# Fused attention, Fourier mixing and feed-forward on one core: the planned cost of the late weight loads, the order of the last chunk, and the planner's constants

## The chip, the cores and the metric

The kernel runs on one core of a Trainium2 chip. The metric is the device time of one execution in microseconds (us). The profile names the engines of the core PE (TensorE, matrix products), PEld (its weight loads, beside PE), DVE (VectorE), ACT (ScalarE), POOL (GpSimd) and SP (SyncE, which here only issues DMAs; SPq is its queue).

## What is computed

Windowed attention over 8 batches, 8 heads, 576 positions and 64 columns a head (half of the heads see the last 32 positions, half every fourth of the last 128), then a two-dimensional Fourier transform whose real part is added, a normalisation over the 512 columns, and a feed-forward block 512 to 2048 to 512 with a residual:

```
scores = where(masks, q @ k.T / sqrt(D), -1e9);  x = softmax(scores) @ v   # heads joined: [8, 576, 512]
X = fft(fft(x, axis=1), axis=2)
u = x + real(X)
un = (u - mean(u)) / sqrt(var(u) + 1e-6)
out = u + relu(un @ w_ch1) @ w_ch2
```

The weights arrive in double precision and are taken apart on the chip. Products that need more than PE's single pass are made of a high and a low half of each operand, in three passes (`PASSES`).

## The kernel before

**An order made while the program is built.** Nothing is issued where the Python text stands. Every operation is given to `add` with its engine, a planned duration, what it reads and writes, and a priority number. At the end `Plan.run` plays the whole program through: at each moment a free engine takes, of its operations whose inputs are there in the plan, the one with the lowest number. The order so found on each engine is the program; on the chip each engine follows it strictly and waits on semaphores. For a DMA the planner counts the issuing engine's cost, a transfer of `nbytes / 2.6e5` us that follows the one before it, some 2.5 us of landing, and at most eight in flight for an engine. So a wrong planned duration does not change what is computed, but puts operations in an order that does not fit the chip. The constants `P_...` and `T_...` are offsets of these priorities (or earliest times) for each kind of work; 12 units of priority stand for one batch of attention in the first half.

**First half.** For each batch b, attention runs over four pairs of heads (`attend_pair`, three blocks each; q, k and v loaded by SP into 3 `tq`, 3 `kb` and 4 `vt` buffers). `mix` does the Fourier part and the normalisation of a batch, at priority 12(b+1) + `P_MIX` + `P_MS[b]` - 10, spread over `P_SPAN` + `P_SS[b]` - 10 units (batches 0 and 1 have their own). `prep_w` loads and takes apart the first 6 of 16 slices of the weights (`wa1`, `wa2`), at `P_W` + 9.45 f. `fill` is the feed-forward of tokens through these 6 slices in the plain way (`up` at L1026, `down` at L1042); its results go through ACT into one of two `row` buffers (`keep_part`, L1060) and by SP to memory (L1061). It is the work that can stand in wherever PE has nothing else.

**Second half.** The other 10 slices are taken two by two, in 5 pairs (`NPAIR`), with a scheme of 7 products in place of 8 for a product of 2 x 2 blocks. `blocks` prepares 14 block sums a pair. 30 of the 70 lie in `right_w` and `left_w`. The other 40 have no room as long as the first half runs: they are written to memory (L1011), and loaded late (the list `later`, L1014), 16 into `late_w` and 24 over the used `wa1` and `wa2`. The tokens come in 9 chunks of 512 (`NCH`). `load_blocks` builds the 7 combinations `xb` of a chunk. `two_tiles(p)` runs the 7 products of pair p into one PSUM bank (`product`, L1365, in the order w1; w0, w4; w5, w2; w6; w3), with a snapshot by ACT after each group (`snap`, L1373), and makes of them 7 operands for the way down (`operand`: ACT L1387, then DVE L1390 or L1394). These lie in 8 seats used in turn: 6 `h` buffers and the two `row` buffers. `down7` is one item of the way down: operand i, one half of the rows, three matmuls (L1473) into the shared sum i, one of seven, each in a PSUM bank; the sums collect over the 5 pairs. Between the groups of products `lower(n)` puts the next n items of the pair before into the program, `LOW` = (3, 3, 3, 3, 2) of its 14. Each matmul group of an item takes a turn, 0.01 of priority, and a product stands `P_UP` turns ahead of its place.

**End of a chunk.** After the last pair, `gather` (L1462) adds shared sums into u2 = s0 + s5, u3 = u2 + s6, u2 = u2 + s4. `finish` makes each of the four output tiles of 128 rows: one DVE instruction over 512 columns (L1105, from u3, or from s0's copy and u2), two over 256 (L1109, from s3 and s4, or s1 and s2), and the stores (L1122 for the last chunk, on SP and ACT). In the last chunk the items of the last pair run in the order `END` = (0, 5, 6, 4, 3, 1, 2), else `ORDER` or `FIRST`.

The planner's figures for one late load, and for SP in general:

```
P * 2048 * ROW          # 262144 bytes, ROW = 0.52
def dma(fn, r, w, prio, nbytes, cost=0.4)
```

## Time and profile before

| | us |
|---|---|
| median of 3 runs | 1077.5 (1075.42 to 1081.26) |
| the profiled execution | 1077.81 |
| its span, first to last instruction | 1076.0 |
| PE busy | 1035.3 (96%) |
| DVE busy | 893.0 (83%) |
| ACT busy | 623.9 (58%) |
| mean granted clock of PE | 0.986 |

Busy times are of the whole span; DMA moved 158 MB at a mean of 147 GB/s. A stretch in which PE is not busy, or in which its granted clock is 0.5, is time that something else than the amount of its work decides. Instruction times are from the profiler; the ends of matmuls are modelled, so that neighbouring matmul groups overlap a little in a timeline: six matmuls of 256 columns follow each other in 0.72 us and are shown with 0.87.

### The profile page before, as it was taken

What the parts mean: (1) busy time and instruction counts of PE and PEld (TensorE: products, weight loads), DVE (VectorE), ACT (ScalarE), POOL (GpSimd) and SP (SyncE); (2) the same over time, 40 slices, a digit from 0 to 9 for tenths busy, and PEclk for the clock granted to TensorE, in tenths of its full rate; (3) what the DMA queues carried; (4) which work ended last, traced back from release to release, by engine and by line L of the source; (5) the groups of instructions that cost most, each with busy time, mean ns of one, the idle gap of its engine ahead of it and who ended that gap; (6) DMA issues with size and microseconds to landing.
All of it is one profiled execution on the core that took longest, in us unless ns stands there. A gap on an engine that the chain in (4) does not pass through costs nothing.

```text
span 1076.0 us, 22711 instructions
## 1 busy us (share of the span) xinstructions
PE 1035.3 (96%) x7876; PEld 965.3 (90%) x7876; DVE 893.0 (83%) x2847; ACT 623.9 (58%) x1588; POOL 211.4 (20%) x278
## 2 busy tenths in 40 slices
PE   7999889999999899999999989999999999999996
PEld 5788679888889798999898889999999999999996
DVE  6689997887878957669988468999898999989886
ACT  5788783657845233345445356666665757565763
POOL 1034405354453445400000000000000000110010
PEclk9899999999999999999999989999999999999998
DMA  9887973675735325254778953323324242333031
GB/s 263 257 267 229 269 207 104 175 227 158 208 92 180 93 79 153 69 168 137 239 250 246 371 137 69 99 60 109 79 80 99 70 114 65 99 80 98 22 108 51
DMA packets 116451, 158.19 MB, mean 147 GB/s; under 512 B 11032, under 2 KB 64472, under 8 KB 116336
## 3 DMA queue, kind: packets, MB, share of 16 engines
q1 hardware_dynamic: 112752, 148.03, 47.8%
q0 software_dynamic: 3040, 8.09, 2.6%
q8 instruction: 62, 1.02, 0.4%
q10 hardware_dynamic: 544, 0.62, 0.2%
q14 instruction: 53, 0.43, 0.1%
HBM read 108.40 MB, written 48.29 MB: 146 GB/s over the span
## 4 chain that ended last, share of the span: by engine, by line
PE 58%; DVE 11%; DMA 5%; ACT 1%; issue 1%; SPq 0%; POOL 0%; DVEq 0%; ACTq 0%
PE ff L1365 16%; PE ff L1026 7%; PE ff L1042 7%; PE mix L1473 5%; PE sc L1473 5%; PE pt L1473 2%; PE ff L1473 2%; PE sc L1042 2%; PE av L1473 2%; PE mix L848 2%; PE av L1026 1%; PE pt L1026 1%; PE mix L802 1%; DMA late_w<-wt 1%; PE sc L586 1%
## 5 line engine op out<-in xcount | busy, mean ns | idle before, releaser
L600 ACT ACTIVATE pm<-pm,mx 96x128 f32<-96x128 f32 x384 | 129.0, 394 | 35.8 <-DVE mx L594 34.7
L1082 POOL DMA_INDIRECT ut<-us,flip_sb x20 | 27.9, 1395 | 543.2 <-ACT h L1387 181.0
L1026 PE MATMUL ff<-ut,wa 128*128 128x256 f32 x936 | 125.5, 286 | 4.3 <-DVE h L1034 4.3
L1026 PEld LDWEIGHTS ff<-ut,wa 128*128 128x128 f32 x936 | 117.5, 191 | 6.3 <-DVE h L1034 4.9
L586 PE MATMUL sc<-kb,tq 128*96 128x256 f32 x384 | 109.6, 398 | 8.1 <-DMA tq<-in_q_dram 5.7
L1042 PE MATMUL ff<-wa,h 128*128 128x512 f32 x468 | 113.0, 392 | 0.0
L594 DVE CUSTOM_DVE_ANT_0 pm<-sc,mask_sb 96x128 f32<-96x128 f32 x384 | 92.3, 280 | 24.2 <-PE sc L586 20.6
L1042 PEld LDWEIGHTS ff<-wa,h 128*128 128x128 f32 x468 | 85.7, 188 | 16.3
L620 PEld LDWEIGHTS av<-vt,ptsb 128*96 128x96 f32 x672 | 69.2, 168 | 16.4 <-issue 4.5
L1148 DVE STREAM_TRANSPOSE ut<-ut 128x512 f32<-128x512 f32 (+1 forms) x76 | 72.5, 983 | 9.9 <-DMA ut<-us 9.6
L620 PE MATMUL av<-vt,ptsb 128*96 128x65 f32 x672 | 72.5, 250 | 7.2 <-DVE xt L632 6.4
L1365 PE MATMUL ff<-xb,left_w 128*128 128x256 f32 x486 | 70.2, 286 | 8.1 <-ACT sb L1373 6.8
L1365 PE MATMUL ff<-xb,wa 128*128 128x256 f32 x540 | 75.7, 281 | 0.5 <-ACT s L1373 0.5
L586 PEld LDWEIGHTS sc<-kb,tq 128*96 128x96 f32 x384 | 55.6, 170 | 19.8 <-issue 5.8
L1365 PEld LDWEIGHTS ff<-xb,left_w 128*128 128x128 f32 x486 | 63.2, 192 | 9.4 <-ACT sb L1373 7.0
L1365 PEld LDWEIGHTS ff<-xb,wa 128*128 128x128 f32 x540 | 68.3, 188 | 0.7 <-ACT s L1373 0.7
L1365 PE MATMUL ff<-xb,late_w 128*128 128x256 f32 x486 | 68.2, 279 | 0.0
L1387 ACT ACTIVATE h<-s 128x256 fp32r<-128x256 f32 x136 | 55.4, 415 | 16.8 <-DVE s L1403 8.5
L1032 ACT ACTIVATE h<-ff 128x256 fp32r<-128x256 f32 x78 | 29.9, 383 | 55.8 <-PE ff L1026 54.5
L1365 PEld LDWEIGHTS ff<-xb,late_w 128*128 128x128 f32 x486 | 61.8, 188 | 0.1
L1060 ACT COPY row<-ff 128x512 f32<-128x512 f32 x26 | 15.2, 586 | 65.1 <-PE ff L1042 53.1
L1034 DVE SCALAR_TENSOR_TENSOR h<-ff,h 128x256 fp32r<-128x256 f32 x78 | 32.7, 419 | 23.1 <-ACT h L1032 22.7
(247 smaller groups left out, 2631.5 us busy)
## 6 DMA issues: line engine op xcount, KB each, us to landing
vt<-in_v_dram SPq DMA_DIRECT2D x32, 390.0 KB
wst<-in_w_dram SPq DMA_DIRECT2D x20, 512.0 KB
wt<-wst SPq DMA_DIRECT2D x40, 256.0 KB
us<-uc SPq DMA_DIRECT2D x36, 257.0 KB
part<-row SPq DMA_DIRECT2D x36, 256.0 KB
ut<-us SPq DMA_DIRECT2D x36, 256.0 KB
ut<-part SPq DMA_DIRECT2D x36, 256.0 KB
kb<-in_k_dram SPq DMA_DIRECT2D x62, 144.0 KB
```

The source lines that it names most:

```text
L586: nc.tensor.matmul(sc()[:QB, 256 * n:256 * n + 256], lhsT=tq()[:, cols], rhs=kb()[:, :, keys], start=True, stop=True,)
L594: nc.vector.tensor_tensor_reduce(pm()[:, i], sc()[:QB, KB * i:KB * i + KB], mask_sb()[:, masks[blocks[i // 2]]], -0.125, 3.0e38, ALU.add, ...
L600: add("ACT", 0.295, lambda i=i: nc.scalar.activation(out=pm()[:, i], in_=pm()[:, i], func=AF.Exp, bias=mx()[:, i:i + 1], scale=-1.0), ((mx ...
L620: add("PE", 0.17, lambda i=i: nc.tensor.matmul(av()[:QB, 65 * i:65 * i + 65], lhsT=pt()[:, i], rhs=vt()[:, i % 2, blocks[i // 2]], start=T ...
L1026: nc.tensor.matmul(z()[:, :n_tok], lhsT=wf()[:, a, kk], rhs=ut()[:, p, kk], start=(kk == 0 and n == 0), stop=(kk == KT - 1 and n == 2),)
L1032: add("ACT", act(n_tok) - 0.03, lambda: nc.scalar.activation(out=h()[:, 0, :n_tok], in_=z()[:, :n_tok], func=AF.Relu), (z,), ((h, 0),), prio)
L1034: add("DVE", dve(n_tok), lambda: nc.vector.scalar_tensor_tensor(h()[:, 1, :n_tok], z()[:, :n_tok], 0.0, h()[:, 0, :n_tok].bitcast(F32), op ...
L1042: nc.tensor.matmul(acc(), lhsT=h()[:, a, P * s:P * s + P], rhs=wf()[:, p], start=(first and n == 0), stop=(last and n == 2),)
L1148: nc.vector.transpose(out=o[back], in_=x[:, g])
L1365: nc.tensor.matmul(up_bank()[:, lo:lo + TOK1], lhsT=ap()[:, a, kk], rhs=xb()[:, j, p, kk], start=(start and k == 0), stop=(k == 5), skip_g ...
L1387: add("ACT", act(TOK1), lambda: nc.scalar.activation(out=ap()[:, 0], in_=src(), func=AF.Relu if relu else AF.Copy), need, (k0,), prio)
L1473: nc.tensor.matmul(acc()[:, TOK1 * half:TOK1 * half + TOK1], lhsT=ap()[:, a, P * half:P * half + P], rhs=wap()[:, q_].rearrange("p k f -> ...
```

## The change

Three things. The late loads (the list `later`) are planned with 0.66 of their bytes in place of 0.52, and with 0.65 us of SP in place of 0.4. In the last chunk the way down of the last two pairs is put together: the pair before the last lowers only its items 0, 6, 4, 5 among the last pair's products (`LOW_END`, two at a time), the last pair's items 0, 6, 5, 4 follow, and then the items 3, 2, 1 of both pairs, one sum after the other. For this the last pair's operands get seven seats of their own, over weights that are not read again. `finish` is taken apart into `end_rows`, `end_sum` and `end_store`, and each output tile gets its terms as the sums come. And some twenty constants of the planner have new values, in both halves. `T_WS` is zero everywhere and delays nothing.

```diff
-P_OP, P_GA, P_LB, P_FI = 2.43, 48.72, -40.68, 47.3
-P_PR = 128.43
-P_UP = 10.35
+P_OP, P_GA, P_LB, P_FI = -15.86, 49.21, -18.09, 56.16
+P_PR = 127.84
+P_UP = 0.2
+T_WS = [0, 0, 0, 0, 0, 0]
-P_SS = [10, 10, 10, 10, 15, 12, 10, 10]
+P_SS = [10, 10, 14, 10, 15, 12, 8, 10]
 LOW = (3, 3, 3, 3, 2)
+LOW_END = (2, 2, 2, 2, 0)
-END = (0, 5, 6, 4, 3, 1, 2)
+HEAD, HEAD_LAST, TAIL = (0, 6, 4, 5), (0, 6, 5, 4), (3, 2, 1)
 FIRST = (0, 6, 5, 3, 4, 1, 2)
...
-P_ST, P_FD, P_WD, P_ST0, P_FD0, P_SPAN0, P_SPAN1 = -4.0, -8.83, -10.91, 0.0, 0.0, 30.0, 18.9
-P_QK, P_V, P_TR, P_MIX, P_SPAN, P_W, P_WF, P_FILL, P_FILLT = -8.0, -5.24, -5.0, 4.32, 9.95, 30, 9.45, 42.52, 12.2
+P_ST, P_FD, P_WD, P_ST0, P_FD0, P_SPAN0, P_SPAN1 = -2.25, -8.83, -10.91, 0.0, 0.0, 30.0, 12.02
+P_QK, P_V, P_TR, P_MIX, P_SPAN, P_W, P_WF, P_FILL, P_FILLT = 12.68, -5.24, -5.0, -5.7, 9.95, 24.8, 9.45, 49.31, 12.2
-T_SEQ, T_CHN, T_STEP, P_SEQ, P_CHN = 10.36, 24.62, 1.0, -4.0, -2.0
+T_SEQ, T_CHN, T_STEP, P_SEQ, P_CHN = 11.54, 24.59, 1.0, -4.0, -2.0
...
-                (there, gate3) if of is late_w else (there,), ((of, ("b", x, 0)), (of, ("b", x, 1))), prio, P * 2048 * ROW))
+                (there, gate3) if of is late_w else (there,), ((of, ("b", x, 0)), (of, ("b", x, 1))), prio, P * 2048 * 0.66, 0.65))
...
+    def end_rows(idx, seat, more, half, prio):
+        t, key, at = seat
         need, get = more
 
         def rows():
+            return at()[:, 0:C].rearrange("p (n d) -> p n d", n=2)
         add("DVE", 0.66, lambda: nc.vector.scalar_tensor_tensor(
+            rows(), get(half), at()[:, C + 1:C + 2], rows(), op0=ALU.mult, op1=ALU.add), need, ((t, ("w", key)),), prio, port=True)
+
+    def end_sum(seat, n, acc, half, before, prio):
+        t, key, at = seat
+        cs = slice(256 * n, 256 * n + 256)
+        add("DVE", 0.36, lambda: nc.vector.scalar_tensor_tensor(
+            at()[:, cs], acc()[:, 256 * half:256 * half + 256], at()[:, C + 1:C + 2], at()[:, cs], op0=ALU.mult, op1=ALU.add),
+            (acc, *before), ((t, ("w", key)), (t, ("done", key, n))), prio)
+        return ((t, ("done", key, n)),)
...
+    def spare_seat(n):
+        of, i, ap = seats[n][:3]
+        return (of, ("b", i, 0)), (of, ("b", i, 1)), lambda: ap().rearrange("p a k f -> p a (k f)")
+
+    last_seats = len(hs_)
+    hs_ += [spare_seat(n) for n in range(7)]
...
+        if c == NCH - 1 and i:
+            x = 0 if i in (1, 2) else 2
+            if i == 5:
+                gather(u2, p1, s[5])
+                gather(u3, u2, s[6])
+            elif i == 4:
+                gather(u2, u2, s[4])
+            if i in (4, 2):
+                for half in range(2):
+                    end_rows(4 * c + x + half, w_of[4 * c + x + half], top_rows if i == 2 else low_rows, half, soon())
+            if i in (1, 2, 3, 4):
+                done = ()
+                for half in range(2):
+                    w = w_of[4 * c + x + half]
+                    done = end_sum(w, i % 2 == 0, s[i], half, done, soon())
+                    if i in (1, 3):
+                        end_store(4 * c + x + half, w)
+            return
...
+            def items(p, got, some, c=c):
+                return [lambda i=i, half=half: down7(c, p, i, got[i], half) for i in some for half in (1, 0)]
+            if c < NCH - 1 or p < NPAIR - 2:
+                todo += items(p, got, ORDER if p else FIRST)
+            elif not ending:
+                todo += items(p, got, HEAD)
+                kept = got
+            else:
+                todo += items(p, got, HEAD_LAST)
+                for i in TAIL:
+                    todo += items(p - 1, kept, (i,)) + items(p, got, (i,))
+        lower(len(todo) if c == NCH - 1 else 0)
```

## Rows read from the trace of the kernel before

**Rows 1.** The page, busy us of each engine, share of the span, instructions

```profile
PE 1035.3 (96%) x7876; PEld 965.3 (90%) x7876; DVE 893.0 (83%) x2847; ACT 623.9 (58%) x1588; POOL 211.4 (20%) x278
```

**Rows 2.** Windows: start:end, length, busy of each engine (instructions), clock, DMA share, GB/s

```profile
0.00:50.00 50.00, 41.73 (x264) 31.55 (x264) 32.52 (x223) 31.16 (x89) 5.75 (x14) 0.93 0.91 259
...
50.00:100.00 50.00, 48.71 (x385) 41.48 (x386) 45.15 (x267) 43.04 (x127) 14.18 (x20) 1.00 0.85 256
...
100.00:150.00 50.00, 42.46 (x312) 34.43 (x311) 48.20 (x263) 40.04 (x114) 19.09 (x23) 0.97 0.91 257
...
600.00:650.00 50.00, 43.19 (x316) 41.83 (x315) 26.51 (x60) 23.18 (x56) 0.74 (x1) 0.90 0.67 216
...
1050.00:1076.00 26.00, 17.57 (x149) 17.37 (x147) 18.04 (x40) 7.65 (x20) 0.00 (x0) 0.88 0.19 52
```

**Rows 3.** PE's waits, whole span, then from 640 on: total, times, longest

```profile
PE sc L586 <- DMA tq<-in_q_dram: 5.7, 2, 4.8
...
PE ff L1365 <- ACT ut L1373: 1.2, 2, 0.6
```

**Rows 4.** Timeline round 616: start, us, engine, line, operation [idle before <-releaser]

```profile
597.42 11.74 SPq L1014 DMA_DIRECT2D late_w<-wt  x16
...
609.56 7.44 SPq L1014 DMA_DIRECT2D wa<-wt  x12
...
617.30 0.32 SPq L1061 DMA_DIRECT2D part<-row  x1
...
619.21 0.32 SPq L1061 DMA_DIRECT2D part<-row  x1
...
610.01 0.59 ACT L1060 COPY row<-sc 128x512 f32<-128x512 f32 x1 [0.26 <-PE sc L1042]
...
611.41 0.59 ACT L1060 COPY row<-sc 128x512 f32<-128x512 f32 x1 [0.33 <-PE sc L1042]
...
622.50 0.42 ACT L1387 ACTIVATE row<-s 128x256 fp32r<-128x256 f32 x1 [8.57 <-DMA part<-row]
...
623.44 1.65 PE L1365 MATMUL ff<-xb,left_w 128*128 128x256 f32 x6 [6.81 <-ACT sb L1373]
```

**Rows 5.** SP's waits from 590 to 640, and a piece of the chain from 596

```profile
SPq L1014 <- DMA late_w<-wt: 6.7, 14, 1.5
...
617.30 5.11 DMA part<-row
```

**Rows 6.** Windows of 5 us behind the hole, columns as in Rows 2

```profile
620.00:625.00 5.00, 1.56 (x7) 1.56 (x8) 0.85 (x3) 1.31 (x3) 0.00 (x0) 0.50 1.08 355
...
625.00:630.00 5.00, 5.00 (x27) 5.00 (x27) 3.41 (x9) 2.40 (x7) 0.00 (x0) 0.54 1.19 195
```

**Rows 7.** Timeline of the end, PE, then DVE (of 15 rows first and last behind 1064)

```profile
1050.63 0.87 PE L1365 MATMUL ff<-xb,wa 128*128 128x256 f32 x6
...
1057.02 0.85 PE L1365 MATMUL ff<-xb,wa 128*128 128x256 f32 x6
...
1063.17 0.88 PE L1473 MATMUL mix<-wa,h 128*128 128x256 f32 x6
...
1066.69 0.88 PE L1473 MATMUL ff<-wa,h 128*128 128x256 f32 x6
...
1061.46 0.43 DVE L1394 TENSOR_TENSOR h<-ut,h 128x256 fp32r<-128x256 f32 x1 [0.21 <-ACT h L1387]
...
1064.16 0.69 DVE L1462 TENSOR_TENSOR ut<-ut,mix 128x512 f32<-128x512 f32 x1 [0.51 <-PE mix L1473]
...
1071.68 0.48 DVE L1109 SCALAR_TENSOR_TENSOR ut<-ff,ut 128x256 f32<-128x256 f32 x1
```

**Rows 8.** Instructions of three lines: duration ns min/median/max, first and last start us

```profile
L1026 PE MATMUL ff<-ut,wa x936: 276/280/473, 152.3 to 514.6; 128*128 128x256 f32 x188
...
L1365 PE MATMUL ff<-xb,late_w x486: 276/277/384, 631.6 to 1049.7; 128*128 128x256 f32 x162
...
L561 SPq DMA_DIRECT2D tq<-in_q_dram x34: 355/583/2285, 1.6 to 281.4; - x34
```

More of the change, by code (lines that the diff above doesn't have):

```diff
@@ L903, in mix, with words_of @@
             fill(ut, (NREST + b // 4 * 2, NREST + b // 4 * 2 + 1), 4 * b + 3)
-    def words_of(rows, three, t, gate, prio):
+    def words_of(rows, three, t, gate, prio, at=0.0):
         def flat(lo, n, dtype):
@@ L948, in halves, with prep @@
             (*need, (of, ("b", i, 0))), ((of, ("b", i, 1)),), prio, port=True)
-    def prep(rows, three, dst, t, gate, prio):
-        get = words_of(rows, three, t, gate, prio)
+    def prep(rows, three, dst, t, gate, prio, at):
+        get = words_of(rows, three, t, gate, prio, at)
         halves(get, (dst, 0, dst), (lambda x: x.rearrange("p (k f) -> p k f", k=KT)) if three else (lambda x: x),
@@ L1089, in prepare, with end_store @@
             u(), part(), scale(), u(), op0=ALU.mult, op1=ALU.add), (pk,), (uk,), prio, port=True)
[L1091 to L1092 removed]
+    def end_rows(idx, seat, more, half, prio):
         t, key, at = seat
[L1094 to L1100 removed]
         need, get = more
         def rows():
[L1104 removed]
+            return at()[:, 0:C].rearrange("p (n d) -> p n d", n=2)
         add("DVE", 0.66, lambda: nc.vector.scalar_tensor_tensor(
[L1106 to L1111 removed]
+            rows(), get(half), at()[:, C + 1:C + 2], rows(), op0=ALU.mult, op1=ALU.add), need, ((t, ("w", key)),), prio, port=True)
[6 more added lines that the diff above has]
+        return ((t, ("done", key, n)),)
+    def end_store(idx, seat):
+        t, key, at = seat
         prio = SOON
[L1113 removed]
+        if idx >= NREST:
             pair = idx - NREST
@@ L1121, in put @@
                     p0 = 64 * e + 32 * turn
-                    queues[e][0].dma_start(out=out[2 * pair + e, lo:lo + 32], in_=u()[p0:p0 + 32])
-                add(queues[e][1], 0.5, put, (uk,), (), prio, 32 * 2048 * ROW)
+                    queues[e][0].dma_start(out=out[2 * pair + e, lo:lo + 32], in_=at()[p0:p0 + 32, 0:C])
+                add(queues[e][1], 0.5, put, ((t, ("w", key)),), (), prio, 32 * 2048 * ROW)
         else:
@@ L1126, in finish @@
                 dma(lambda b=b, lo=lo, p0=p0, n=n: nc.sync.dma_start(
-                    out=out[b, lo:lo + n], in_=u()[p0:p0 + n]), (uk,), (), prio, n * 2048 * ROW)
-        return [(t, ("done", key, n)) for n in range(2)]
+                    out=out[b, lo:lo + n], in_=at()[p0:p0 + n, 0:C]), ((t, ("w", key)),), (), prio, n * 2048 * ROW)
+    def finish(idx, seat, more, accs, half, before, last):
+        prio = SOON + 0.001 * (last + P_FI)
+        end_rows(idx, seat, more, half, prio)
+        done = [end_sum(seat, n, acc, half, (before[n],) if before else (), prio)[0] for n, acc in enumerate(accs)]
+        end_store(idx, seat)
+        return done
     def words(t):
@@ L1412, in two_tiles @@
         snap(ys, TOK1)
-        lower(LOW[0])
+        lower(low[0])
         product(0, w[0], 0, True)
@@ L1420, in two_tiles @@
         got[0] = operand(s1, ((sa, "n"),), True)
-        lower(LOW[1])
+        lower(low[1])
         product(0, w[5], 4, False)
@@ L1428, in two_tiles @@
         got[6] = operand(v2, ((sb, "u"),), False)
-        lower(LOW[2])
+        lower(low[2])
         product(0, w[6], 5, False)
@@ L1438, in two_tiles @@
         got[5] = operand(s1, ((sa, "n"),), False)
-        lower(LOW[3])
+        lower(low[3])
         product(0, w[3], 6, False)
@@ L1444, in two_tiles @@
         got[2] = operand(s21, (s21,), False)
-        lower(LOW[4])
+        lower(low[4])
         return got
@@ L1504, in fused_kernel @@
         for p in range(NPAIR):
-            got = two_tiles(p)
+            ending = c == NCH - 1 and p == NPAIR - 1
+            if ending:
+                last_turn[0] = 0
+            got = two_tiles(p, LOW_END if ending else LOW)
             marks[c, p] = Buf(ap=0)
@@ L1511, in fused_kernel @@
                     prepare(idx, w_of[idx], soon(P_PR), (c, PR_AT))
-            todo += [lambda c=c, p=p, i=i, got=got, half=half: down7(c, p, i, got[i], half)
-                     for i in (END if c == NCH - 1 and p == NPAIR - 1 else ORDER if p else FIRST) for half in (1, 0)]
-    lower(len(todo))
+            def items(p, got, some, c=c):
[5 more added lines that the diff above has]
+                kept = got
+            else:
+                todo += items(p, got, HEAD_LAST)
+                for i in TAIL:
+                    todo += items(p - 1, kept, (i,)) + items(p, got, (i,))
+        lower(len(todo) if c == NCH - 1 else 0)
     plan.run()
```

62 lines of the change are left out of this document (24 added, 38 removed).

## The prediction

> **What bounds the kernel now.** I read the page's busy times first, then the span cut into stretches, then who waited for whom on TensorE (PE in the rows), then the timeline round each hole. PE is busy 1035.3 of 1076.0 us [rows 1], so all its idle time is 40.7 us; the change removes no matmul, so it can only win idle time or time at the lower clock. The stretches show where that is [rows 2]: 8.3 us in the first 50, 1.3 in the next, 7.5 from 100 to 150, 6.8 from 600 to 650 and 8.4 in the last 26. Of PE's waits, one of 6.8 us on ScalarE (ACT) is the largest [rows 4], then comes the first load with 4.8; after 640 the longest is 0.6 [rows 3].
>
> **The hole at 616 us.** ACT copies the last two fill results into the two `row` buffers at 610.01 and 611.41, done at 610.6 and 612.0. Their stores sit in SyncE's (SP's) order behind 28 late weight loads, which begin at 597.42, and go out only at 617.30 and 619.21 [rows 4]. The next writer of the first `row` buffer is an operand of the first pair, and ACT, which runs in order, stands in front of it for 8.57 us, with PE's next snapshot (L1373) queued behind it. So PE has nothing for 6.81 us, from 616.63 until 623.44 [rows 4]. The clock then pays too: it is 0.50 from 620 to 625 and 0.54 from 625 to 630 [rows 6], that is 1.2 instead of 2.4 GHz until about 629.6. PE ran from 623.44, so (629.6 - 623.44)/2 = 3.1 us are lost beside the 6.8: together 9.9 us.
>
> Why the planner put the stores there: it counts 262144 bytes times 0.52 over 2.6e5, or 0.524 us, and 0.4 us of SP for each load. The 28 loads took 11.74 + 7.44 = 19.18 us, 0.685 each [rows 4]. At the end of them the planner's clock is 28 x (0.685 - 0.524) = 4.5 us early, so in its plan the loads are through before the `row` copies are. SP's own waits say that it is the transfers: SP waited 14 times for an earlier late load to land, 6.7 us in sum [rows 5].
>
> **The change, part by part.**
>
> *Late loads.* The new figures are 0.665 us of transfer and 0.65 of SP. Now the planner errs by 28 x 0.02 = 0.6 us. When the copies end, about ten loads are still to go; the stores have a far lower priority number and take the next place, one load (0.69) later: 611.3 and 612.7. Their landing I leave at the measured 5.11 us [rows 5], because the same loads surround them: `row` is free at 616.4 and 617.8 in place of 622.4 and 624.5. PE came 0.94 us after ACT's `row` operand (622.50 to 623.44). If only the first `row` operand stands before the snapshot, PE resumes at 617.4, 0.8 us after it ran dry; if both do, at 618.8, 2.2 after. For the clock behind so short a hole I have bounds alone, 0 and half of the 3.1. Residue 0 to 3.8, taken as 1.3, since the planner may also put the snapshot first. Gain 9.9 - 1.3 = 8.6 us, ends 6.1 and 9.9. The late loads themselves move back by two stores of 0.32 us issue; their readers start at 631.6 [rows 8], or 8 us earlier without the hole, while the first `late_w` load left at 597, so what hides it is that lead; gone, it would cost a landing of 5 us.
>
> A page speaks against the size of this. The Trainium skill ("DMA: Bandwidth & Descriptors", section "Issuing engines are not separate DMA queues") says that all queues end in the same 16 DMA engines and that starting a transfer is usually short beside the transfer. By that, a store sent earlier still has to share the engines with the loads. The trace agrees as far as the waits on landing go; by the rule alone only the queue time is won, and that is the end with a residue of 3.8, a rival below.
>
> *Order of the last chunk.* Before, the DVE tail hangs on the shared sum 5 of the last pair: its matmuls start at 1063.17, DVE starts at 1064.16 and works through 15 instructions (3 gathers, 4 of 512 columns, 8 of 256) to 1072.16; PE is done at 1067.57; the end is 1076.0 after the last stores [rows 7]. The naive gain: only two additions of 0.39 remain after the last matmul, so the end comes at about 1068.6 + 3.8, 3.6 us earlier. But the 15 instructions all stay, and all of them wait, directly or through a gather, for sums 5 and 6. They take 8.0 us from the moment 5 is done, so the question is only when that is. Sum 5 needs its operand, and this comes from the product with w6 (1057.02, end 1057.87): its low half is written from 1061.46 to 1061.89 [rows 7], 4.0 us after w6; PE then still finished the pair before and ran sum 0, so 5 was done 6.2 us after w6. With those behind it the wait falls to 4.0 + 0.2 + 0.72 = 4.9 us. Against that, `P_UP` goes from 10.35 to 0.2 turns. With 10.35 a product overtakes about three items (an item is half a sum, three matmuls, three turns); 16.9 us of PE work lay after the pair's first product at 1050.63, that is 7 products and 33 items of 0.36. Now 28 items lie after it (8 + 6 of the pair before, 14 of its own), so that product starts 5 x 0.36 = 1.8 us later against the end of PE. From first product to sum 5 I get 0.72 + 1.44 + 1.44 + 0.72 of products, three gaps of 0.75 to 0.9 and the 4.9: 11.8 us, where it was 13.4. So 1.6 won and 1.8 lost. The final stores of both halves now become due within 0.39 us, so up to 0.8 us may be lost in the two queues; 0.8 of idle inside the DVE chain may be won. Ends -1.5 and +3.6, taken +0.5, near the chain, because the chain's rows are those that end last.
>
> *Constants of the first half.* Mixing of batches 2 to 7 gets 10 units earlier, the first weights' preparation 5.2, fill 6.8 later, q and k loads 20.7 later (12 units are one batch). PE has no fill before 152.3 [rows 8], and in the first 150 us it idles 17.1 of them, 4.8 of which are the first load [rows 2, 3]. In 100 to 150 DVE is busy 48.2 of 50 [rows 2], so it is work for PE that is short, not PE. The q loads of the 96 units of attention spread over 1.6 to 281.4 us [rows 8], so a unit is about 2.9 us and preparation ends perhaps 15 us earlier: fill could take a third of the other 12 idle microseconds, 4. The same DVE work then presses on the stretch from 50 to 100, where PE idles only 1.3. Bounds: all 12 won, or as much lost again as the stretch from 100 to 150 now has, 7.5. I take +2, between the third and that pressure.
>
> *Constants of the second half.* There is little to win: the largest group of waits after 640 is 1.2 us in two places [rows 3]. `P_UP` leaves fewer items in hand behind a chunk's last product (16 instead of 22, 5.8 instead of 7.9 us of PE work) for the rebuilding of `xb`; `P_LB` makes that rebuilding no more urgent than the operands (-18.1 and -15.9, against -40.7 and 2.4). Eight chunk changes at 0 to 0.6 us, the longest wait there now: ends +1.2 and -4.8, taken -0.6, near what the rows show today.
>
> Sum: 8.6 + 0.5 + 2 - 0.6 = 10.5 us off the profiled execution's 1077.8 us (span 1076.0 and 1.8 round it; the median of the runs is 1077.5, so 0.3 is all that separates them): 1067.3, said as 1067.5.
>
> **Rivals.**
> First, the store lands no sooner than the shared engines let it: residue 3.8 and no help from the rest, gain 6.1 + 0.5 - 0.6 = 6 or less, so 1071 to 1073. For it: the DMA share is 1.08 and 1.19 in the hole's ten microseconds [rows 6]. Against: most of the lost time was queue time, not transfer. By the rule of the Trainium skill named above ("DMA: Bandwidth & Descriptors", the same section) this is the case to expect.
> Second, the hole moves instead of closing: in the new order another ACT or SP instruction stands before a late landing (the snapshot behind the second `row`, or the next chunk's input), or the early stretches lose what the hole gives: 1073 to 1079. For it: every order is new, and the planner's durations differ from the chip's elsewhere too. Against: in before, no other wait after 640 is above 0.6 [rows 3].
> Third, slower. The q and k loads of batches 1 to 7 fall by 20.7 units, nearly seven pairs of heads at three units each, behind stores and weights in SP's choice, with DMA at 0.85 to 0.91 of its time from 0 to 150 [rows 2]. Three buffers give a lead of two pairs, 2 x 3 x 2.9 = 17 us. If the lead is used up at every batch, PE pays a load each time, 4.8 us as at the start [rows 3], 7 x 4.8 = 34 at most; taken at half, 1067.5 + 17 = 1084. It decides from where a load leaves later than the scores of the pair before it; then `sc <- DMA tq` grows well over its 5.7 us. Against: SP picks whatever is ready, and a load whose buffer is free waits only for a gap of SP, and its lead is long beside the 0.5 us that SP spends on one.
> Fourth, more: the tail at its better end and the early idle halved, 1058 to 1062.
>
> **How the numbers follow.** Forecast (1063 to 1071): 0.52. First rival 0.14, second 0.15, third 0.07, fourth 0.12. A measurement of this kernel tells about 0.5%, 5.4 us, from no change: the bounds are 1072.1 and 1082.9. Faster: the forecast, the fourth, two thirds of the first and little of the second, 0.73; same: 0.20; slower: the third, 0.07. The range leaves out the third, half of the second and the far end of the fourth: 1059 to 1076.
>
> **What would show it.** Right: in the stretch round the switch to the second half the two `row` stores stand among the late loads, no wait of PE above 2.5 us, clock 1.00 in 620 to 630. Tail: last DVE addition 4 to 5 us after the last matmul (naive: 1 to 1.5). First half: fill begins before 145 us and the idle time of 100 to 150 is under 7.5. Wrong, if PE's sum of idle and slow time before 600 us has grown by more than 5 us, or a wait on q and k appears.

## The result and the profile after

After the change the kernel takes 1069.6 us (median of 8 runs, 1068.34 to 1072.13), the kernel before 1078.57 in the runs beside it (8 runs, 1074.97 to 1084.78). The ratio is 0.9917, 95% interval 0.9892 to 0.9941: faster by 9.0 us, with 6.4 and 11.6 as ends. The forecast was 1067.5, range 1059 to 1076. The profiled execution after took 1068.3 us, span 1066.5, against 1077.8 and 1076.0 before.

The page after, columns as in [rows 1], and then its windows, columns as in [rows 2]:

```profile
PE 1030.0 (97%) x7876; PEld 962.6 (90%) x7876; DVE 889.7 (83%) x2847; ACT 621.7 (58%) x1588; POOL 216.0 (20%) x278
```

```profile
0.00:50.00 50.00, 34.79 (x205) 25.32 (x206) 36.85 (x201) 28.07 (x76) 5.75 (x14) 0.89 0.90 271
50.00:100.00 50.00, 47.69 (x356) 39.48 (x355) 43.12 (x247) 41.32 (x123) 12.37 (x16) 0.98 0.80 240
100.00:150.00 50.00, 47.93 (x394) 42.98 (x392) 48.42 (x256) 40.94 (x118) 22.21 (x26) 1.00 0.77 224
600.00:650.00 50.00, 47.30 (x369) 46.24 (x368) 33.97 (x76) 28.94 (x69) 0.00 (x0) 0.97 0.66 209
...
615.00:620.00 5.00, 4.03 (x23) 4.03 (x24) 3.33 (x9) 2.91 (x8) 0.00 (x0) 0.66 1.05 397
620.00:625.00 5.00, 5.00 (x45) 5.00 (x44) 2.60 (x7) 3.32 (x9) 0.00 (x0) 1.00 1.24 182
...
650.00:1050.00 400.00, 398.98 (x3350) 396.36 (x3349) 359.80 (x825) 255.15 (x612) 28.02 (x18) 1.00 0.32 83
```

Busy time is not the best measure here. In the first 50 us PE is idle 15.2 us where it was 8.3 [rows 2], from 100 to 150 it is idle 2.1 where it was 7.5, and up to 600 us the idle time is 23.7 against 23.6: nothing seems won. But both programs issue 7876 matmuls, and counting those done is plainer. To 150 us there were 955, before 961 (the sums of the rows here and in [rows 2]); to 600 us 4101 against 4075; from 600 to 650 369 against 316; from 650 to 1050 3350 against 3341. The second half at full pace does 423 in 50 us (700 to 750 us before), 0.118 us each. At this pace 26 matmuls or 3.1 us came before 600, 53 or 6.3 us at the change from the first to the second half, and 9 or 1.1 us after. The tail gave 0.7 back (below); together 9.8, and the spans differ by 9.5. This splits the difference of two traces, and the one after is of the fastest of its 8 runs; how far the count to 600 us scatters is shown with the experiments. The row of before for the long stretch:

```profile
650.00:1050.00 400.00, 398.14 (x3341) 395.21 (x3341) 360.94 (x827) 258.99 (x614) 25.86 (x18) 1.00 0.33 84
```

PE's longest waits after, over the whole span (total us, times, longest):

```profile
PE sc L588 <- DMA tq<-in_q_dram: 5.9, 2, 4.5
PE pt L615 <- ACT pm L602: 5.3, 1, 5.3
PE ff L1378 <- ACT sb L1386: 2.7, 1, 2.7
```

The third is what is left of the hole [rows 4]. The wait on q is where it was [rows 3]. The second is new and stands in the first 50 us, from 43.2 to 48.5. The timeline round the hole after (start, us, engine, line, operation, idle before and what ended it):

```profile
594.45 11.82 SPq L1016 DMA_DIRECT2D late_w<-wt  x16
606.63 3.01 SPq L1016 DMA_DIRECT2D wa<-wt  x5
609.96 0.32 SPq L1063 DMA_DIRECT2D part<-row  x1
610.62 0.32 SPq L1016 DMA_DIRECT2D wa<-wt  x1
611.26 0.32 SPq L1063 DMA_DIRECT2D part<-row  x1
...
606.27 0.59 ACT L1062 COPY row<-sc 128x512 f32<-128x512 f32 x1 [0.26 <-PE sc L1044]
607.33 0.57 ACT L1062 COPY row<-sc 128x512 f32<-128x512 f32 x1
...
615.03 0.42 ACT L1402 ACTIVATE row<-s 128x256 fp32r<-128x256 f32 x1 [4.46 <-DMA part<-row]
...
615.97 1.65 PE L1378 MATMUL ff<-xb,left_w 128*128 128x256 f32 x6 [2.70 <-ACT sb L1386]
```

The two stores now stand between the late loads, after 21 and 22 of them instead of after 28 and 30, counted from the first load into `late_w` [rows 4]. But the first still left 3.1 us after its copy was done (606.86 to 609.96). ACT's operand, which waited for its landing, started 5.07 us later, and PE resumed 0.94 us after that, with the same pattern as before. The granted clock was 0.50 from 616 to 618 and 0.55 from 618 to 619, so (618.9 - 615.97)/2 = 1.5 us go with the 2.70 of idle time: 4.2 us where there had been 9.9.

The end after, PE and then DVE:

```profile
1040.81 0.87 PE L1378 MATMUL ff<-xb,wa 128*128 128x256 f32 x6
...
1047.13 0.87 PE L1378 MATMUL ff<-xb,wa 128*128 128x256 f32 x6
...
1053.18 0.87 PE L1488 MATMUL mix<-wa,right_w 128*128 128x256 f32 x6
...
1056.53 0.87 PE L1488 MATMUL mix<-wa,right_w 128*128 128x256 f32 x6
...
1054.09 0.69 DVE L1477 TENSOR_TENSOR ut<-ut,mix 128x512 f32<-128x512 f32 x1 [0.77 <-PE mix L1488]
...
1061.15 0.86 DVE L1105 SCALAR_TENSOR_TENSOR ut<-mix,ut 128x256 f32<-128x256 f32 x2
```

Here the picture is that of before [rows 7]: sum 5 starts 6.05 us after w6 (1047.13 to 1053.18; it was 6.15), DVE then works through its 15 instructions in 7.92 us (it was 8.00), and its last ends 4.61 us after the last matmul (it was 4.59). From there to the end of the span it is 4.49 us, where it was 3.84.

### The profile page after: what moved, and what is told of

It is laid out like the page before. It is cut to its first block, busy times and chain, and to the rows that moved or that the text cites. A ratio compares the mean times of both kernels' runs of the same rounds, so it can differ in the third digit from the quotient of the medians.

```text
span 1066.5 us, 22708 instructions
## 1 busy us (share of the span) xinstructions
PE 1030.0 (97%) x7876; PEld 962.6 (90%) x7876; DVE 889.7 (83%) x2847; ACT 621.7 (58%) x1588; POOL 216.0 (20%) x278
## 4 chain that ended last, share of the span: by engine, by line
PE 81%; DVE 11%; DMA 4%; ACT 1%; issue 1%; SPq 1%; DVEq 0%; ACTq 0%
PE ff L1378 19%; PE ff L1028 9%; PE ff L1044 9%; PE sc L1488 5%; PE sc L588 5%; PE mix L1488 5%; PE av L622 4%; PE mix L850 3%; PE pt L1488 3%; PE mix L804 3%; PE av L1488 3%; PE ff L1488 3%; PE sc L1044 2%; DVE pm L596 2%; PE pt L615 2%; PE av L1028 1%
## 5 line engine op out<-in xcount | busy, mean ns | idle before, releaser
L588 PE MATMUL sc<-kb,tq 128*96 128x256 f32 x384 | 107.2, 393 | 7.4 <-DMA tq<-in_q_dram 5.9
L1402 ACT ACTIVATE h<-s 128x256 fp32r<-128x256 f32 x134 | 54.9, 416 | 12.7 <-DVE s L1418 5.3
L618 ACT COPY ptsb<-pt 128x384 f32<-128x384 f32 x84 | 39.6, 472 | 25.7 <-PE pt L615 16.4
```

The lines of the kernel that those rows point to most:

```text
L588: nc.tensor.matmul(sc()[:QB, 256 * n:256 * n + 256], lhsT=tq()[:, cols], rhs=kb()[:, :, keys], start=True, stop=True,)
L618: add("ACT", act(4 * QB) - 0.05, lambda: nc.scalar.copy(out=pt().rearrange("p i q -> p (i q)"), in_=ps()[:, :4 * QB]), (ps,), (pt,), prio)
L1402: add("ACT", act(TOK1), lambda: nc.scalar.activation(out=ap()[:, 0], in_=src(), func=AF.Relu if relu else AF.Copy), need, (k0,), prio)
```

## The experiments

Each kernel was set against the kernel before. For each I read three things from its trace: T1, the start of the first product of the second half; the time from T1 to the end of the span; and the tail, from the last matmul to the last DVE instruction and from there to the end. The last column has the matmuls done to 600 us, from 600 to 650 and from 650 to 1050. "Old" and "new" figures mean the planner's two numbers for a late load, 0.524 us of transfer and 0.4 of SP, or 0.665 and 0.65.

| kernel | T1 | T1 to end | matmul to DVE | DVE to end | median | ratio, 95% | matmuls |
|---|---|---|---|---|---|---|---|
| before | 597.9 | 478.1 | 4.59 | 3.84 | 1078.57 | 1 | 4075, 316, 3341 |
| after | 594.2 | 472.3 | 4.61 | 4.49 | 1069.60 | 0.9917 (0.9892 to 0.9941) | 4101, 369, 3350 |
| e1_late | 596.6 | 478.0 | 4.58 | 4.04 | 1076.79 | 0.9991 (0.9975 to 1.0007) | 4087, 360, 3300 |
| e2_last | 598.2 | 478.7 | 3.41 | 4.38 | 1078.18 | 0.9990 (0.9972 to 1.0007) | 4074, 324, 3322 |
| e3_const | 596.1 | 478.2 | 4.81 | 4.57 | 1075.28 | 0.9956 (0.9940 to 0.9973) | 4089, 314, 3353 |
| e4_first | 597.9 | 472.1 | 4.61 | 4.33 | 1071.96 | 0.9947 (0.9927 to 0.9966) | 4075, 365, 3349 |
| e5_actq | 597.4 | 472.3 | 4.61 | 4.43 | 1070.84 | 0.9922 (0.9898 to 0.9947) | 4080, 365, 3347 |
| e6_up | 597.5 | 472.5 | 4.61 | 4.21 | 1071.25 | 0.9927 (0.9902 to 0.9953) | 4079, 377, 3333 |
| e7_qk | 603.7 | 467.9 | 4.61 | 4.40 | 1074.42 | 0.9957 (0.9938 to 0.9977) | 4050, 388, 3338 |
| e9_late_up | 599.3 | 475.1 | 4.57 | 3.97 | 1074.81 | 0.9963 (0.9947 to 0.9978) | 4070, 361, 3318 |
| e10_more | 597.6 | 467.0 | 4.03 | 4.23 | 1065.98 | 0.9875 (0.9851 to 0.9899) | 4078, 400, 3351 |
| e11_tail | 600.7 | 467.0 | 4.02 | 4.06 | 1065.29 | 0.9870 (0.9846 to 0.9894) | 4058, 395, 3350 |
| e12_oldend | 597.2 | 468.0 | 4.78 | 4.00 | 1066.12 | 0.9878 (0.9850 to 0.9906) | 4082, 400, 3347 |
| e13_one | 597.4 | 473.2 | 4.03 | 4.44 | 1072.05 | 0.9931 (0.9909 to 0.9952) | 4080, 362, 3338 |

Each ratio is to runs of the kernel before made beside that kernel, whose medians were 1077.65 to 1079.59, so the ratios can be compared and the medians only roughly. T1 is a weak measure: kernels with the same constants of the first half show it from 594.2 to 600.7, so one trace of each tells nothing finer than some 3 us. T1 to end repeats within 0.2 us where the second half is planned alike (after and e4_first, 472.3 and 472.1). The times decide where they differ by more than their intervals.

### The late loads alone

e1_late is the kernel before with the new figures, nothing else:

```diff
-                (...), prio, P * 2048 * ROW))
+                (...), prio, P * 2048 * 0.66, 0.65))
```

> The kernel before with the late loads' planned figures (0.66 of the bytes, 0.65 us) as the only edit. Theory A (the late loads are the larger half of the gain, by way of the two row stores): the stores leave some four to six loads earlier, PE's wait behind the ACT row operand falls from 6.8 to 2.5-3.5 us, the slow clock behind it from 6.2 to about 3 us of matmul time, 5 to 6 us in all: ratio 0.995. Rival B (the constants of the first half and the order of the last chunk make the whole gain): within 0.2% of before, the hole only moves.

SP's queue and PE's wait in e1_late, and two of its windows, columns as before:

```profile
609.00 3.08 SPq L1014 DMA_DIRECT2D wa<-wt  x5
612.43 0.32 SPq L1061 DMA_DIRECT2D part<-row  x1
...
614.30 0.32 SPq L1061 DMA_DIRECT2D part<-row  x1
```

```profile
PE ff L1365 <- ACT sb L1373: 3.2, 1, 3.2
```

```profile
600.00:650.00 50.00, 46.80 (x360) 45.47 (x360) 32.23 (x72) 27.87 (x66) 0.00 (x0) 0.97 0.67 214
...
650.00:1050.00 400.00, 395.72 (x3300) 390.80 (x3299) 356.41 (x818) 256.19 (x605) 30.06 (x18) 1.00 0.32 83
```

The stores moved forward as said and the hole shrank from 6.8 to 3.2 us. From 600 to 650 it did 44 matmuls more than before (360 against 316, 5.2 us). Yet T1 to end is 478.0, and the ratio's interval holds 1. The window behind tells why: 3300 matmuls from 650 to 1050 where before did 3341, 41 fewer, or 4.8 us. They are missing in thin slices, 26 of them from 850 to 950 (816, before 842). So the hole's gain was real and was given back over the next 400 us: with the late loads planned longer, the old constants make another order of the second half, and that is a worse one. That was foreseen by neither theory.

### The order of the last chunk alone

e2_last is the changed kernel with the old figures for the loads and the old priorities:

```diff
-... prio, P * 2048 * 0.66, 0.65))
+... prio, P * 2048 * ROW))
-P_OP, P_GA, P_LB, P_FI = -15.86, 49.21, -18.09, 56.16
+P_OP, P_GA, P_LB, P_FI = 2.43, 48.72, -40.68, 47.3
...
```

> The order of the last chunk alone, with all constants and the late loads' figures of before. Theory A (15 vector instructions hang on shared sum 5, so the order wins nothing, and two halves of output due together cost some 0.6 us in the store queues): time from PE's last matmul to the end 8.5 to 9.3 us, before 8.4; ratio 0.999 to 1.001. Rival C (only the last sum's two additions remain behind the last matmul): 4.9 us from the last matmul to the end, 3.6 us less time, ratio 0.9966.

PE's and DVE's rows of the end of e2_last:

```profile
1058.55 0.85 PE L1378 MATMUL ff<-xb,wa 128*128 128x256 f32 x6
...
1063.61 0.64 PE L1488 MATMUL mix<-wa,right_w 128*128 128x256 f32 x4
...
1068.24 0.87 PE L1488 MATMUL mix<-wa,right_w 128*128 128x256 f32 x6
...
1064.61 0.68 DVE L1477 TENSOR_TENSOR ut<-ut,mix 128x512 f32<-128x512 f32 x1
...
1071.65 0.87 DVE L1105 SCALAR_TENSOR_TENSOR ut<-mix,ut 128x256 f32<-128x256 f32 x2
```

Alone the order does what the prediction said of it: sum 5 starts 5.06 us after w6 instead of 6.15, DVE is done 3.41 us after PE instead of 4.59, and its 15 instructions still take 7.9. Of these 1.2 us the stores take back 0.5 (DVE to end 4.38 against 3.84), and T1 to end is 478.7 against 478.1. The ratio is 1 within its interval: the naive gain of 3.6 us is out.

### The new constants alone

e3_const is the kernel before with all of the new priorities, but the old figures for the loads and the old order of the last chunk:

```diff
-P_OP, P_GA, P_LB, P_FI = 2.43, 48.72, -40.68, 47.3
-P_UP = 10.35
+P_OP, P_GA, P_LB, P_FI = -15.86, 49.21, -18.09, 56.16
+P_UP = 0.2
...
```

> The kernel before with all the new constants, but with the late loads' old figures and the old order of the last chunk. Theory A: the first half ends 3 to 4 us earlier, the hole at the switch stays at 5.5 to 7 us, the rest moves by under 1 us: ratio 0.996 to 0.998. Rival B: ratio 0.992, the constants alone give the whole gain. Rival D (the constants fit only the new figures): 1.000 or slower.

PE's longest wait in e3_const:

```profile
PE ff L1365 <- ACT sb L1373: 7.9, 1, 7.9
```

With the old figures the hole is there, 7.9 us of it, and T1 to end stays at 478.2, although 3353 matmuls are done from 650 to 1050 where before did 3341. The ratio 0.9956 says that the constants give 4.7 us by themselves (2.9 to 6.5), though the one profiled execution shows only 1.7 (span 1074.3 against 1076.0). That lies just under theory A's ratio; rivals B and D are out.

### Everything but the first half's constants

e4_first is the changed kernel with `P_ST` to `P_SPAN1`, `P_QK` to `P_FILLT`, `T_SEQ`, `T_CHN` and `P_SS` as before:

```diff
-P_QK, P_V, P_TR, P_MIX, ... = 12.68, -5.24, -5.0, -5.7, 9.95, 24.8, 9.45, 49.31, 12.2
+P_QK, P_V, P_TR, P_MIX, ... = -8.0, -5.24, -5.0, 4.32, 9.95, 30, 9.45, 42.52, 12.2
...
```

> The changed kernel with the first half's constants of before (P_SS, P_ST, P_SPAN1, P_QK, P_MIX, P_W, P_FILL, T_SEQ, T_CHN). Theory A: the first product of the second half comes at 597 to 599 us in place of 594, the hole stays closed to under 3.5 us: 3 to 4 us over the changed kernel, ratio to before 0.995. Rival B: all gone, ratio 0.999 to 1.001.

T1 to end is 472.1, that of the changed kernel; T1 is that of before. So the second half has its whole gain without the first, and the first half's constants are worth what remains: 0.9917/0.9947 is 0.30%, 3.2 us, though with both intervals anything from nothing to 6.7. The matmul count to 600 us agrees for the traces of before and after alone (26 more, 3.1 us). Over all traces it does not: the eight kernels with the new constants of the first half had done 4058 to 4101 by then, 4081 in the mean, and the five with the old ones 4070 to 4087, in the mean 4076 (e7_qk has some of each and is left out). That is 5 matmuls or 0.6 us. So the times speak for a gain in the first half, and its size stays open.

With these four the second half can be laid out by two of the parts (T1 to end, us):

| | old figures for late loads | new figures |
|---|---|---|
| old constants of the second half | 478.1 (before) | 478.0 (e1_late) |
| new constants | 478.2 (e3_const) | 472.3 (after), 472.1 (e4_first) |

Neither part alone moves it; together they take 6 us. The matmuls of the first table say where: the new figures bring 44 to 55 from 600 to 650 with either set of constants, but cost 41 from 650 to 1050 with the old constants and 3 with the new. (After and e4_first also have the new order of the last chunk, which is worth 0 to 1 us: e2_last above and e12_oldend below.)

### Which constant lets the gain through

e9_late_up adds to e1_late only the new `P_UP`; e6_up is the changed kernel with the old one:

```diff
-P_UP = 10.35
+P_UP = 0.2
```

> The kernel before with two edits, the late loads' figures and P_UP = 0.2. Theory E: the hole falls to 2.5-3.5 us as with the late figures alone, and the second half keeps it: ratio to before 0.9945 to 0.9965. Rival H: as the late figures alone, 0.998 to 1.000.

> The changed kernel with P_UP back at 10.35, so that products overtake three items again. Theory E (the late figures pay only with P_UP near 0: with 10.35 the second half runs with many short waits on snapshots, as the run of the late figures alone did, 41 fewer matmuls from 650 to 1050): 3 to 5 us over the changed kernel, ratio to before 0.995 to 0.997. Rival H (the loss in that run came from the other constants): within 1 us of the changed kernel, 0.991 to 0.993.

Added to the late figures alone, `P_UP` = 0.2 takes T1 to end from 478.0 to 475.1, half of the way; from 650 to 1050 there are 3318 matmuls against 3300 in e1_late. Taken out of the changed kernel it seems to cost nothing: 472.5 against 472.3, and the ratios 0.9927 and 0.9917 lie in each other's intervals. By the ratios theory E holds in e9_late_up and rival H in e6_up. But in the trace of e6_up two things cancel. Its longest wait in the second half, and two of its windows:

```profile
619.36 0.98 PE L1378 MATMUL ff<-xb,left_w 128*128 128x256 f32 x6 [1.95 <-ACT s L1386]
```

```profile
600.00:650.00 50.00, 47.71 (x377) 46.17 (x376) 33.28 (x74) 28.22 (x66) 0.33 (x1) 1.00 0.73 231
...
650.00:1050.00 400.00, 398.59 (x3333) 394.95 (x3332) 358.45 (x824) 254.67 (x610) 32.90 (x18) 1.00 0.32 83
```

From 650 to 1050 it does 17 matmuls fewer than the changed kernel, 2.0 us, as many as `P_UP` brought in e9_late_up (18). From 600 to 650 it does 8 more: PE ran dry 19.9 us after T1 in place of 19.1, stood 1.95 us in place of 2.70, and the granted clock stayed at 1.00. So in the long stretch `P_UP` is worth about 2 us with the old constants round it and with the new, and the other new constants bring 32 or 33 matmuls, 3.9 us. Which of those does it was not tried, and stays open.

### The two stores on another queue

e5_actq is the changed kernel with the last two `row` stores issued by ACT, right behind its copies, so that no planner's figure stands between copy and store:

```diff
-    dma(lambda: nc.sync.dma_start(out=parts[idx](), in_=row()), ...)
+    add("ACT", 0.5, lambda: nc.scalar.dma_start(out=parts[idx](), in_=row()), ...)
```

> The changed kernel with the last two row stores issued from ACT's queue, right behind the copies that fill them, so that SP's 40 late loads stand before none of them. Theory A (queue time is the rest of the hole): the stores leave at 607 and 608 in place of 610 and 611.3, land about 5 us later, at 612 to 613, because the late loads still fill the DMA engines; PE's wait falls from 2.7 to under 1 us, no slow clock behind it: 3 to 4 us under the changed kernel, ratio to before 0.988 to 0.989. Rival F (what is left is transfer, the store shares the engines with eight loads whenever it leaves): landing grows to 7 or more, the wait stays above 2 us, time as the changed kernel, 0.992.

SP's queue, ACT and PE in e5_actq, and a step of its chain of waits (start, us, what):

```profile
610.15 9.69 SPq L1016 DMA_DIRECT2D wa<-wt  x14
620.42 0.96 SPq L1084 DMA_DIRECT2D ut<-us  x2
...
610.04 0.40 ACTq L1066 DMA_DIRECT2D part<-row  x1
...
615.10 0.42 ACT L1405 ACTIVATE row<-s 128x256 fp32r<-128x256 f32 x1 [1.46 <-DMA part<-row]
...
626.86 0.72 ACT L1090 ACTIVATE ut<-ut 128x512 f32<-128x512 f32 x1 [2.96 <-DMA ut<-us]
...
628.10 1.65 PE L1381 MATMUL ff<-xb,late_w 128*128 128x256 f32 x6 [2.48 <-ACT sb L1389]
```

```profile
620.42 6.42 DMA ut<-us
```

The first store left at 610.04, right behind its copy, and the first hole is gone (clock 1.00 from 615 to 620). It still took about 5.0 us to land: issued by ACT it lost its queue time, and its landing stayed what it was. The Trainium skill ("DMA: Bandwidth & Descriptors", section "Issuing engines are not separate DMA queues") states that transfers run on the same 16 DMA engines whichever engine started them; the landing that stayed agrees. But ten microseconds later PE stands for 2.48 us behind another SP transfer: the two `ut<-us` loads, which bring the next chunk's input, now left behind all 14 `wa` loads, at 620.42, which is 23.0 us after T1 (in the changed kernel 615.56, 21.4 after T1), and their landing took 6.42 us. In the changed kernel the first hole sets PE back by 4.2 us, which can hide such a wait. T1 to end is 472.3 once more, which neither theory had foreseen: theory A has the first hole right, and the ratio is rival F's. This is the second rival, the hole that moves, made by hand: freeing one transfer from the late loads leaves the next one behind them.

### More planned time for a late load

If the queue behind the loads is the cause, a larger planned figure than the measured one should go on gaining, until products are held back for loads that are there already. e10_more plans 0.8 and 0.8, e13_one 1.0 and 1.0, else as the changed kernel:

```diff
-... prio, P * 2048 * 0.66, 0.65))
+... prio, P * 2048 * 0.8, 0.8))
```

> The changed kernel with the late loads planned still longer, 0.8 of the bytes and 0.8 us, so that the two row stores stand behind 13 loads into late_w, 8 places earlier than in the changed kernel. Theory A: SP waits some 3 us for the copies, the stores land by 612, PE's wait is under 1 us: ratio to before 0.988 to 0.990. Rival G (the figures have an optimum at the measured ones, and later loads now come too late for the third pair): a new wait of PE on a late load of 2 us or more, ratio 0.992 or above.

> The changed kernel with 1.0 of the bytes and 1.0 us for a late load: the two row stores stand ahead of all 16 loads into late_w, which now come last. Theory A (any figure that keeps the row stores and the next chunk's input ahead of the loads' tail will do): as with 0.8, ratio 0.987 to 0.989. Rival G (a figure above the measured 0.7 makes the planner wait for loads that have long landed, or brings late_w too late for the third pair): PE waits 3 us or more on a load or behind ACT after 620, ratio 0.991 or above.

SP's queue in e10_more round the change of halves, and its windows there:

```profile
600.48 9.53 SPq L1016 DMA_DIRECT2D late_w<-wt  x13
610.42 1.23 SPq L1063 DMA_DIRECT2D part<-row  x2
611.73 1.63 SPq L1016 DMA_DIRECT2D late_w<-wt  x3
...
616.28 0.94 SPq L1081 DMA_DIRECT2D ut<-us  x2
```

```profile
600.00:650.00 50.00, 50.00 (x400) 48.89 (x399) 35.76 (x81) 31.15 (x75) 0.40 (x1) 1.00 0.72 233
...
630.00:650.00 20.00, 20.00 (x172) 20.00 (x171) 19.97 (x43) 13.51 (x34) 0.00 (x0) 1.00 0.19 64
```

Both stores go out in the pause after the `late_w` loads, the first 0.16 us after its copy ends (609.67 + 0.59), the input loads follow at 616.28, and PE has no idle time at all from 600 to 650, at full clock. T1 to end falls by 5.3 to 467.0; the residue of 4.2 and about 0.8 us of tail account for most of it. The ratio is 0.9875 (0.9851 to 0.9899), a little better than theory A's 0.988 to 0.990; no wait on a late load appears. Its interval just touches that of the changed kernel, but e11_tail and e12_oldend, with the same figures, lie at 0.9870 and 0.9878: 0.8 beats both kernels.

The second of these windows in e13_one:

```profile
630.00:650.00 20.00, 17.30 (x135) 16.01 (x134) 16.71 (x33) 8.30 (x20) 0.00 (x0) 1.00 0.42 142
```

With 1.0 the planner believes the late loads late, and SP still issues some at 627 to 636. There is no hole at 616, but from 630 to 650 135 matmuls run where e10_more has 172, 4.4 us of work less. PE runs no product from 628.0 to 635.7, only items of the way down, and then stands up to 0.9 us at a time for snapshots. So theory A is out; the ratio is rival G's, though no single wait reaches its 3 us. Four planned figures, T1 to end: 0.524 gives 478.2 (e3_const, with the old order of the last chunk), 0.665 472.3, 0.8 467.0, 1.0 473.2. The best of the four is above the measured 0.70 to 0.72, not at it. The figure for the bytes and that for SP were moved together; which of them matters was not tried.

### The end, twice more

e12_oldend is e10_more with the old order of the last chunk (the code before, all new constants, 0.8 and 0.8). e11_tail is e10_more with the last tiles' additions sorted by tile, so that each tile's store can leave sooner:

```diff
-            if i in (1, 2, 3, 4):
+            if i in (1, 3, 4):
...
+                    if i == 1:
+                        done = end_sum(w, 1, s[2], half, done, soon())
```

> The kernel before with all new constants and 0.8 of the bytes and 0.8 us for a late load, so it differs from the run with these figures in the order of the last chunk alone. Theory A (the order wins nothing, the 15 vector instructions behind shared sum 5 set the end either way): from the first product of the second half to the end 466.5 to 467.6 us, from PE's last matmul to the end 8.3 to 9.4, ratio to before 0.987 to 0.989. Rival C (the order wins the naive 3.6 us, hidden so far by run to run scatter): 470 to 471 us, ratio 0.990 to 0.992.

> The kernel with 0.8 of the bytes and 0.8 us for a late load, and at the end each of the last two output tiles gets its two additions (sums 2 and 1) one behind the other, so that the first tile's stores fall due 0.8 us before the second's in place of 0.4. Theory A (the two tiles' stores stand in each other's way in the queues): from the last vector instruction to the end 4.0 to 4.2 us in place of 4.4 to 4.6; time within 0.5 us of the kernel without it, ratio to before 0.987. Rival (the stores' landing alone counts): 4.4 to 4.6, no change.

Old against new order at 0.8: T1 to end 468.0 against 467.0, ratios 0.9878 and 0.9875. The order is worth up to 1 us in a trace and nothing that the times can show; rival C is out. e11_tail cuts DVE to end from 4.23 to 4.06, and the time is e10_more's within the interval.

### q and k loads as urgent as before

e7_qk is the changed kernel with `P_QK` = -8.0, as before:

```diff
-P_QK, P_V, ... = 12.68, -5.24, ...
+P_QK, P_V, ... = -8.0, -5.24, ...
```

> The changed kernel with P_QK back at -8, q and k loads as urgent as before. Theory A (the loads have lead enough, P_QK matters little): PE's wait on q loads 5.5 to 6.2 us as in both kernels, first half within 1.5 us of the changed kernel's, ratio 0.991 to 0.993. Rival 3 of the prediction (late q and k loads cost the first half something): first half shorter by 2 us or more, ratio 0.989 or less. Rival I (the late q and k loads are what lets the weights and stores through): longer by 2 us or more, ratio 0.994 or more.

Two windows of e7_qk:

```profile
0.00:50.00 50.00, 42.55 (x279) 32.20 (x279) 35.45 (x236) 33.21 (x95) 5.76 (x14) 1.00 0.92 274
...
100.00:150.00 50.00, 41.68 (x258) 32.81 (x256) 43.91 (x219) 33.33 (x92) 14.84 (x19) 0.83 0.75 217
```

Urgent q and k loads win the first 50 us, 279 matmuls against 205, and pay for it from 100 to 150, 258 against 394, with DVE busy 43.9 instead of 48.4 and the clock at 0.83. To 600 us there are 4050 matmuls, fewer than in any other kernel, and the ratio 0.9957 is behind the changed kernel's 0.9917. So rival I holds: with the other new constants, demoting these loads helps. (T1 and T1 to end can't be compared for this kernel: its first products stand later among the last fill. In all the others the copy of the first `row` result is done 12.6 to 12.7 us after T1, here 9.9 us. From that copy to the end it is 458.1 us, in the changed kernel 459.7, in e10_more 454.4. There is no hole: the stores leave behind three `late_w` loads, and no wait of PE in the second half is above 0.5 us. So the place of the stores depends on where the first half's work falls, too.)

## Why the prediction was right, point by point

**The total.** Forecast 10.5 us off, measured 9.0 (6.4 to 11.6); 1067.5 against 1069.6, inside the forecast's own 1063 to 1071. That it came so near is in part luck. Set beside the split of the two traces above, the hole brought 2.9 us less than said (2.3 by matmuls) and the last chunk 1.2 less, the first half 1.1 more and the rest of the second half 1.7 more, and these misses mostly cancel. Nor are they four separate gains, as the runs show (below).

**The hole.** The mechanism was right: in every kernel with larger figures that leaves the stores with SP they stand among the late loads, and the hole shrinks or goes. The term was mis-sized, 8.6 said, 5.7 measured (9.9 - 4.2). The step that failed is "now the planner errs by 0.6 us", from which the stores were to leave one load, 0.7 us, after their copies; the first left 3.1 us after. In the plan, with 0.65 us of SP for each load, it stands at least 21 x 0.65 = 13.65 us behind the first load into `late_w`. On the chip the 21 loads took 15.51 us (594.45 to 609.96), 0.74 each with a pause, so the planner was 1.9 us early; and the copy was done 12.41 us after that first load (606.86), 1.2 us before the plan has the store. Together these are the 3.1. The rows before already held the sign: there the store left 6.7 us after its copy (610.6 to 617.30 [rows 4]), and the planner's error on the loads explained 4.5 of them. The other 2.2 were taken as cured, too. In all five kernels with these figures and SP's stores 2.7 to 3.2 us are left. The landing, 5.11 taken, measured about 5.0, was right, and so was 0.94 from ACT's operand to PE. For the clock behind a short hole I had only bounds, 0 and 1.6; it paid 1.5, near the upper. The residue of 4.2 lies just above its bound of 3.8, so for this term the first rival had the better number. Its reason does not hold, though: what was left to win was queue time, as e5_actq and e10_more show, which closed this hole with the loads still around it, in e5_actq with the landing unchanged. Of the 8.2 us from the copy's end to ACT's operand in the changed kernel 5.1 were landing and 3.1 queue, and taking the 3.1 away was enough, since PE ran dry only 1.8 us before that operand started (613.27 and 615.03). The rule of the Trainium skill weighed there ("DMA: Bandwidth & Descriptors", same section) agrees with the landing that did not shrink, and says nothing of waiting behind other transfers in an issuing queue.

**The constants of the second half.** -0.6 was said, as if they acted by themselves. By themselves they do little (e3_const: 478.2 against 478.1, with a hole 1.1 and a tail 0.95 us longer, so about +2; the 12 matmuls more from 650 to 1050 are 1.4). But without them the new figures for the loads are worth nothing (e1_late). The prediction added the terms; the runs show that two of them are no sum. That was the one thing that could have cost the whole gain at the hole, and the wait list before [rows 3], on which the -0.6 rested, could not show it: it lists what one order waits for, not what another would.

**The order of the last chunk.** +0.5 was said. Alone it brought the 1.1 us at sum 5 (1.3 said), of which the stores took 0.5 back (up to 0.8 said); in the changed kernel, with all constants, 6.05 us from w6 to sum 5 are back, so that nothing is left: 9.10 us from the last matmul to the end against 8.43. The loss foreseen from `P_UP` was the wrong one: from the last pair's first product to PE's end there are 16.59 us, 32 items, where it was 16.94 and 33.3; 1.3 items less, not five, so 0.35 us and not 1.8. What sum 5 waited for was DVE, which in the changed kernel brings the operand for sum 5 only 4.6 us after w6's snapshot (1048.41 to 1052.99; e2_last 3.65). The naive gain of 3.6 was rightly refused.

**The constants of the first half.** +2 was said, within the bounds; the times give 3.2 (nothing to 6.7), the matmuls of the two traces 3.1, those of all traces 0.6. So the runs neither bear the size out nor refute it. The way was in part the one told: the first fill matmul came at 121.8 us instead of 152.3 ("before 145" was said):

```profile
L1028 PE MATMUL ff<-ut,wa x936: 276/280/473, 121.8 to 510.8; 128*128 128x256 f32 x188
```

and 100 to 150 has 394 matmuls where it had 312. That the first 50 us would lose 59 matmuls for it was not foreseen, and the idle time of the first 150 us, which the prediction counted as what can be won, grew from 17.1 to 19.6 us.

**The third rival** (q and k loads too late, 1084) did not come, and had the sign wrong: `sc <- DMA tq` went from 5.7 to 5.9 only, and putting the loads back makes the kernel slower (e7_qk).

**The signs to look for.** Right: the stores among the loads, clock 1.00 from 620 to 630, DVE 4 to 5 us behind PE, fill before 145, idle under 7.5. Wrong: a wait of 2.7 us where 2.5 was the limit, and the slow clock stood in 615 to 620 (0.66), where I had not looked.

## What to carry to other kernels

Where a planner orders DMA issues, a transfer planned too short puts whatever is issued next behind a queue that the plan believes empty; look for transfers that another engine waits for and that leave late behind many others, and try a little more than the measured time: too short costs a hole and too long holds work back (here 0.8 beat the measured 0.7, and 1.0 lost it all again). Check that a planner's error explains the whole of a delay before counting the whole as won. Two changes to one order don't add: try each alone and with the other, since a gain at one place can be given back in thin slices over the rest. And measure progress by the instructions done up to a time, not by busy time, and in more than one trace.

## What the runs showed of the hardware

A store of 262144 bytes took 5.0 to 5.1 us to land among back-to-back loads of the same size, issued by SP (before, after) or by ACT (e5_actq), and the next chunk's input, two loads of about that size, took 6.4 us behind them (e5_actq). One late load followed the other every 0.69 to 0.72 us; from 615 to 620 us after the change the DMA engines moved 397 GB/s in all. An idle time of 2.70 us at 613.3 to 616.0 was followed by a clock of 0.50 until about 618.9, three microseconds of half pace for less than three of idleness; behind the hole of 6.8 us before, it was about six [rows 4, 6]. After 1.95 us of idle time at the same place in e6_up it stayed at 1.00.
